# Local attention with memory readout and a gated MLP: the order of issue written out as a table, and five settings of steps

## The chip, the core and the metric

The kernel runs on one core of one Trainium2 chip. The core's engines each take their instructions in the order in which the program lists them: TensorE (PE in the profile, with its weight loads as PEld), VectorE (DVE), ScalarE (ACT), GpSimd (POOL) and SyncE (SP, which here only issues transfers). An instruction that waits for another engine or for a transfer holds back all that stands behind it on its own engine. The metric is the device time of one execution in microseconds, the median of several runs.

## The reference

Attention over B=4 batches, H=8 heads, S=576 positions and D=64, mixed with a readout of a memory matrix, and then a gated MLP over the 2304 tokens:

```python
scores = where(causal, -1e9, q @ k.T / sqrt(D))
a = exp(scores - scores.max(-1)); a /= a.sum(-1) + 1e-9
local = a @ v
q_p = where(q > 0, q, exp(q) - 1) + 1                      # phi
mem_out = (q_p @ M_prev) / ((q_p @ z_prev) + 1e-6)
x = g * mem_out + (1 - g) * local                          # g = sigmoid(beta), by head
xn = x / sqrt(mean(x * x) + 1e-6) * rms_g                  # x as 2304 x 512
out = (silu(xn @ w_gate) * (xn @ w_val)) @ w_out           # 512 -> 1536 -> 512
```

The inputs come as float64 words for the weights and float32 for q, k, v; the result is float32.

## The kernel before

The 2304 tokens are 18 row blocks of 128, numbered in the order in which they are worked on: 0 to 3 are the first rows of the four batches, 4 to 9 are rows 1 to 3 of batches 0 and 1 in turn, 10 holds the 64 last rows of both, 11 to 13 are rows 1 to 3 of batch 2, 14 to 16 those of batch 3, 17 the last rows of both. Two blocks make one of nine chunks of 256 tokens for the MLP. Blocks 0 to 3 and chunk 0 are computed in float32; all later ones split each operand into a high and a low float16 part and add three matmuls.

Attention goes by units of one block and one or two heads (four in blocks 0 to 3). A unit's score matmuls (`u_scores`, L480) are masked, scaled and reduced to a row minimum by DVE (L486); ACT takes the exponential (L545) and writes the high part of P (L547); the low part P lo is a subtraction (`u_lo`): on DVE (L563), or on POOL (L567) for the blocks that `NPOOL` names, of which those that get a P lo are 4 to 7. On POOL's way a small DVE addition (L494) shifts the row minimum first. Then the SP queue issues one transposing transfer for both parts (PT, L569), and TensorE multiplies it with v (`u_pv`, L600 to L602). The score banks (tag sc) and the gate/value banks (tag gv) in PSUM have two buffers each, PT has four.

For each block q, k, phi(q) and x are split into two parts and transposed by transfers on the SP queue (qT, kT, phT, xT); qT needs two more copies inside SBUF (L385, L386), which wait in the queue for its transpose. v is split by `prep_v` with `VWAY`: "1" is a scaling pass and a cast on ACT (L125, L129) and a subtraction on POOL (L132); "0" is one scaling cast on ACT (L108) and a multiply-subtract on DVE (L111).

The MLP of a chunk has twelve gate/value projections (`m_proj`, 24 matmuls L959 each, or L952 in float32 in chunk 0) and twelve down projections (`m_down`, L1029 to L1031). `m_act` (L975, L976, L979) turns a projection's bank into h and so frees it. The weights are converted from float64 words (L871, L875, L881) and split (L111) during the first chunks; `C1` is how many pieces of the second third of d_ff are converted ahead of the first projections, `E0` how many projections of chunk 1 go ahead of the split of w_out.

The statistics of a batch need gram matmuls (`gram`, csum, L167); `GDE` names, for the first two batches, the event that they are held back for (x0 and x1: the RMS scale of block 0 and of block 1 is done). The preparation of a block is a list of steps (st), each emitted at a place that a planner chooses by costs; `o` shifts some steps of the second rows of batches 2 and 3. The program is emitted in that planner's order with priorities, and the framework's scheduler sets the final order on each engine by those priorities and its own estimate of times.

Of the kernel before, what the change touches and what calls it, by code (L numbers as in the profile page):

```python
# [29 lines left out]
SP = ((2, 0), (2, 4))  # L30
GDE = ("x1", "x1")
GDL = ("x1", "x1")
# [3 lines left out]
T32 = "aaadd"  # L36
C1 = 8
E0 = 8
HEADA = 0.4
D1 = 4  # L40
D2 = 8
SPLIT = ("0", "0", "033", "0")
VWAY = "11"
HLAG = 3
# [22 lines left out]
GP = -600  # L67
NPOOL = (2, 8)


@with_exitstack
def attn_memory_moe_kernel(
# [12 lines left out]
    nc = tc.nc  # L85
# [4 lines left out]
    P = 128  # L90
# [13 lines left out]
    ps = ctx.enter_context(tc.tile_pool(name="ps", bufs=2, space=bass.MemoryType.PSUM))  # L104


    def hi_cast(dst, src, scale):
# [26 lines left out]
    def pow2_scales(ssq, n, s_out, inv_out):  # L134
# [9 lines left out]
        nc.vector.reciprocal(s_out, inv_out)  # L144

    def over_partitions(src, n):

        t = ps.tile([P, 512], F32, tag="sc", name="allp")
        nc.tensor.matmul(t[:n, :P], src, ident, start=True, stop=True)
        v = tiny.tile([P, 1], F32, tag="vmax", name="vmax", bufs=1)  # L150
        nc.vector.tensor_reduce(v[:n], t[:n, :P], axis=AX.X, op=ALU.max)
        nc.tensor.matmul(t[:, P : P + n], v[:n].to_broadcast([n, P]), ident[:n, :n], start=True, stop=True)
        return t[:, P : P + n]

    def total(src, n):

        t = ps.tile([P, 512], F32, tag="sc", name="allp")
        nc.tensor.matmul(t[:, :n], mhalf[:, 1:2].to_broadcast([P, P]), src, start=True, stop=True)
        return t[:, :n]
# [65 lines left out]
    zs = const.tile([P, 4], F32, name="zs")  # L225

    def load_kv(n, ev=""):
        tag = "kvt" if is_tail[n] else "kv"
        stage[n] = sb.tile([P, 2, HD], F32, tag=tag, name=f"kv{n}", bufs=1 if is_tail[n] else 4)
        for j in range(2):  # L230
            ins = nc.sync.dma_start(out=stage[n][:, j], in_=qkv[at_row[n], :, j, :])
            if ev:
                after(ins, event[ev])


    def load_M(b):
        if b < 2:
            held["M", b, 0] = held["M", b, 1] = NF - b + 100
            qst[("M", b)] = wo[:, NF - b, :]
        else:  # L240
            qst[("M", b)] = sb.tile([P, HD], F32, tag="q", name=f"M{b}")
        for hf in range(2):
            nc.sync.dma_start(
                out=qst[("M", b)][hf * D : (hf + 1) * D], in_=M_prev[b].rearrange("d h e -> d (h e)")
            )
# [3 lines left out]
    def spare(name):  # L249
        t = sb.tile([P, H, VW], F16, tag="v16", name=name, bufs=10)  # L250
        return t.bitcast(F32).rearrange("p a b -> p (a b)")[:, :HD]

    def load_32(n):
        kv32[n] = []
        for j in range(2):
            kv32[n].append(spare(f"kv32_{n}_{j}"))
            nc.sync.dma_start(out=kv32[n][j], in_=qkv[at_row[n], :, j, :])
        b = blocks[n][0]
        qst["M32", b] = spare(f"M32_{b}")
        for hf in range(2):  # L260
            nc.sync.dma_start(
                out=qst["M32", b][hf * D : (hf + 1) * D], in_=M_prev[b].rearrange("d h e -> d (h e)")
            )

    def src32(n, j):
        return stage[n][:, j] if n < 2 else kv32[n][j]

    def load_q(n):
        if n in qst:
            return  # L270
        qst[n] = sb.tile([P, HD], F32, tag="q", name=f"q{n}")
        nc.sync.dma_start(out=qst[n], in_=qkv[at_row[n], :, 2, :])
# [7 lines left out]
    def stat_begin(b):  # L280
        stt[b] = tiny.tile([P, 3, NI + 1], F32, tag="stt", name=f"stt{b}", bufs=2)
        nc.gpsimd.memset(stt[b], 0.0)

    def stat_blk(b, i):
        if b < 2:
# [18 lines left out]
        else:  # L304
            n = blk_of[(b - b % 2, NI)]
            r0 = (b % 2) * TR
            for j in range(2):
                square_acc(stage[n][r0 : r0 + TR, j], stt[b][r0 : r0 + TR, j, NI : NI + 1])

    def stat_M(b):  # L310

# [5 lines left out]
        del held["M", b, 0]  # L317

    def stat_end(b):
        if b >= 2:  # L320
# [16 lines left out]
        if b % 2 == 1:  # L337
# [3 lines left out]
            tcb[b // 2] = t  # L341

    def prep_M(b):
        src = (qst.pop if b >= 2 else qst.get)(("M", b)).rearrange("p (h e) -> p h e", h=H)
# [21 lines left out]
    qsc = {}  # L366

    def q_stats(n):
        ss = tiny.tile([P, 2], F32, tag="ss", name="ss", bufs=2)
# [4 lines left out]
        pow2_scales(ss, 2, sc[:, 0:2], sc[:, 2:4])  # L374

    def q_consts(n):
        c, sc = consts_of(n), qsc[n]

        nc.vector.tensor_tensor(sc[:, 4:6], sc[:, 1:3], c[:, 6:8], ALU.mult)

    def prep_q(n):
        t = split_rows(qst[n], qsc[n][:, 0:1], RWAY[0])
# [3 lines left out]
        nc.sync.dma_start(out=qT[n][:D, 1], in_=qT[n][D:, 0])  # L386

    def phi_calc(n):

# [6 lines left out]
        qst[n] = ph  # L396

    def prep_phi(n):
        t = split_rows(qst.pop(n), qsc[n][:, 1:2], RWAY[1])
        phT[n] = sb.tile([P, H, P], F16, tag="phT", name=f"phT{n}", bufs=1)  # L400
        tposed(phT[n], t)

    def transposed(dst, src, on_act):

# [18 lines left out]
    def prep_qk32(n):  # L423
# [3 lines left out]
        transposed(q32[n][:, 0], qst[n], T32[1] == "a")  # L427

    def prep_phi32(n):
        transposed(q32[n][:, 1], qst.pop(n), T32[2] == "a")  # L430

    def prep_k(n):
        c = consts_of(n)
        t = split_rows(stage[n][:, 0], c[:, 0:1], RWAY[2])
        kT[n] = sb.tile([P, H, P], F16, tag="kT", name=f"kT{n}", bufs=10)
        tposed(kT[n], t)

    def prep_v(n):
        c = consts_of(n)
# [9 lines left out]
    def group(n):  # L449
        return max(1, 4 // (blocks[n][1] + 1)) if blocks[n][1] < 2 else 1  # L450

    def u_scores(n, h0):
        b, i = blocks[n]
# [43 lines left out]
    def tail_scores(n, h, s, nm, t, w):  # L497
# [29 lines left out]
        Ssb[(n, h)] = (s, w + P, nm0)  # L527

    def u_exp(n, h0):
        s, w, nm = Ssb[(n, h0)]  # L530
# [12 lines left out]
        for g in range(G):  # L543
            v_ = s[:, g * w : (g + 1) * w]
            nc.scalar.activation(v_, v_, AF.Exp, bias=nm[:, g : g + 1], scale=-1.0)  # L545
        p16 = sb.tile([P, 2 * (NI * P + P)], F16, tag="P16", name="P16", bufs=2)
        nc.scalar.activation(  # L547
            p16[:, : G * w], s[:, : G * w], AF.Copy, scale=PSCALE if not lo_on_pool(n, h0) else 1.0
# [3 lines left out]
    def lo_on_pool(n, h0):  # L552
        return NPOOL[0] <= n < NPOOL[1]

    def u_lo(n, h0):
        if n < NA:
# [17 lines left out]
    def after(ins, ev):  # L574
# [4 lines left out]
        )  # L579

    def u_pv(n, h0):
        b, i = blocks[n]
# [40 lines left out]
    pairs = {}  # L623

    def pair_memory(pr):

# [9 lines left out]
        pairs[pr] = mb, zb  # L636

    def pair_M(b):

# [5 lines left out]
        if b < 2:  # L645
            del held["M", b, 1]

    def mem32(n):

# [17 lines left out]
        nc.vector.tensor_tensor(t1s[n], acc, f.unsqueeze(2).to_broadcast([P, H, D]), ALU.mult)  # L667

    def pv32(n, h0, pt):
        b, i = blocks[n]  # L670
        if h0 == 0:
            accs[n] = ps.tile([P, 2, 4, D], F32, tag="a1", name=f"loc{n}", bufs=1)
        for g in range(group(n)):
# [5 lines left out]
            )  # L679

    def evac32(n, g4):
        f = den.pop((n, g4))
# [10 lines left out]
        event["e%d%d" % (n, g4)] = nc.gpsimd.tensor_tensor(part, part, t2, ALU.add)  # L693

    def mem_mm(n, g4):
        if n < NA:
# [23 lines left out]
        for (bb, r), acc in zip(halves, found):  # L720
# [4 lines left out]
            )  # L725

    def loc_evac(n, g4):
        if n < NA:
# [27 lines left out]
    xdone = {}  # L756

    def x_norm(n):
        x = t1s[n].rearrange("p h d -> p (h d)")
# [6 lines left out]
        t1s[n] = (x, ss)  # L766

    def x_float(n):

# [11 lines left out]
        )  # L781

    def x_split(n):
        if n < 2:
# [36 lines left out]
    def hold(p, at):  # L821
# [3 lines left out]
        return wo[:, at : at + 2, :].rearrange("p a f -> p (a f)")  # L825

    def load_w(m, cc, t):
        w = (w_gate, w_val)[m]
# [11 lines left out]
    def in_wgv(at):  # L840
        return wgv[:, at : at + 2, :].rearrange("p a f -> p (a f)")

    def load_pre(b, i):

        pre[(b, i)] = []
        for j in range(2):
# [4 lines left out]
            pre[(b, i)].append(t)  # L851

    def load_wo(f):
        at = {0: 7, 1: 9, 2: 11, 3: 7, 4: 9, 5: 11, 7: 9, 9: 11}.get(f)
# [9 lines left out]
    event = {}  # L864

    def f64_to_f32(raw, dst, p):

# [21 lines left out]
    wos = const.tile([P, NT3 + 8], F32, name="wos")  # L889

    def gv_scales(t):

# [23 lines left out]
        )  # L916

    def wo_scales():

# [7 lines left out]


    def w_split(m, cc, t):
        p = piece(m, cc, t)  # L930
        src = wgv[:, p + 1, :]
        sc = rgs[:, t, m, cc : cc + 1]
        split(wgv16[:, p, :512], wgv16[:, p, 512:], src, sc, way_of(SPLIT, t, p % (2 * NC)))

    def wo_split(f):
        src = wo[:, f + 1, :]
# [3 lines left out]
    gvp, h16s, outp = {}, {}, {}  # L940

    def m_proj(F, m):
        c, f = F // NF, F % NF
# [4 lines left out]
        for cc in range(NC):  # L948
# [9 lines left out]
            for lhs, rhs in ((whi, cc), (whi, NC + cc), (wlo, cc)):  # L958
                nc.tensor.matmul(o, lhs, xT[c][:, rhs, :], start=(cnt == 0), stop=(cnt == 3 * NC - 1))  # L959
                cnt += 1  # L960

    def m_act(F):
        if F < NF:
# [19 lines left out]
        h16s[F] = th  # L983

    def m_split(F):
        if F < NF:
# [10 lines left out]
        h16s[F] = h16  # L997

    def put(c, tb, scale):
        if tb == 0:  # L1000
# [7 lines left out]
        for p0, np_, b, s0 in rows_of(2 * c + tb):  # L1008
            (nc.scalar).dma_start(out=out[b * S + s0 : b * S + s0 + np_, :], in_=res[p0 : p0 + np_])

    def m_down(F):
        c, f = F // NF, F % NF
# [21 lines left out]


    def setup_small():
        nc.scalar.dma_start(out=beta_sb, in_=beta.rearrange("(o h) -> o h", o=1).to_broadcast([P, H]))
# [4 lines left out]
    gmax2 = const.tile([P, 1], F32, name="gmax2")  # L1042

    def setup_gain():

# [3 lines left out]
        nc.vector.tensor_tensor(gmax2, gmax2, gmax2, ALU.mult)  # L1049

    def setup_consts():

# [21 lines left out]
    def prep_steps(n):  # L1074

        b, i = blocks[n]
        st = [[] for _ in range(8)]
        o = 2 if i == 1 and b >= 2 else 0
        if n < NA:
# [138 lines left out]


    def w_conv(i):  # L1220
        m, cc, t = pcs[i]
# [3 lines left out]
        for nx in NEXT.get(i, ()):  # L1225
            load_w(*pcs[nx])

    def wo_conv(f):
        f64_to_f32(raws.pop(("o", f)), wo[:, 1 + f, :], len(pcs) + f)
# [88 lines left out]
    a_until(1e9)  # L1318
    downs(NCHUNK * NF, 99)


# [59 lines left out]
```

## Time and profile before

| | us |
|---|---|
| median of 3 runs | 638.47 |
| the runs | 644.07, 637.28, 638.47 |
| the profiled execution | 637.33 |
| its span in the trace | 635.5 |
| PE busy | 600.3 |
| DVE busy | 444.5 |
| ACT busy | 405.3 |
| POOL busy | 175.3 |

The span is the time between the first and the last recorded instruction; the profiled execution's own time is 1.8 us longer. The busy time of PE counts the modelled ends of pipelined matmuls. Idle time of an engine is put down to whatever ended it.

### The profile page before, as it was taken

The page shows a single profiled execution, that of the slowest core. Times are in us where ns is not written, and L with a number is a line of the kernel's source. Part 1 is how long each engine was busy: PE and PEld are TensorE (multiplying, and loading weights), DVE is VectorE, ACT ScalarE, POOL GpSimd, SP SyncE. Part 2 cuts the span into 40 slices and gives each one's busy share as a digit, 9 for nine tenths or more (in the row PEclk, how much of TensorE's full clock was granted, in tenths as well). Part 3 has the DMA queues.
Part 4 walks back from the last instruction along what each step waited for, and adds up shares of the span by engine and source line. Part 5 has one row for each costly group of instructions (what it writes and reads, how often), then busy time and mean ns, then how long its engine had stood idle before and what let it go on. Part 6 is the DMA issues. An engine that isn't in the chain of part 4 may idle for free. (4 is left out here: it accounts for less than half of the span.)

```text
span 635.5 us, 15913 instructions
## 1 busy us (share of the span) xinstructions
PE 600.3 (94%) x6092; PEld 473.0 (74%) x6092; DVE 444.5 (70%) x1301; ACT 405.3 (64%) x874; POOL 175.3 (28%) x263
## 2 busy tenths in 40 slices
PE   5889999998899999999999988889999999999996
PEld 4778876777667788888778766667777878887774
DVE  3858886887997668676977667687876757852222
ACT  4687994978887667675755664886665645432321
POOL 2220010228865343222212521152222222022111
PEclk9969999999999999999999999999999999999999
DMA  7996652478877776785597467549856444430001
GB/s 254 352 393 248 224 188 83 77 177 192 159 144 155 133 153 145 145 167 90 61 179 144 96 132 151 130 88 177 161 109 112 85 85 92 80 64 18 34 1 34
DMA packets 183788, 87.58 MB, mean 138 GB/s; under 512 B 165792, under 2 KB 165792, under 8 KB 183712
## 3 DMA queue, kind: packets, MB, share of 16 engines
q1 hardware_dynamic: 180640, 81.82, 57.9%
q10 hardware_dynamic: 3072, 4.74, 2.4%
q8 instruction: 48, 0.79, 0.5%
q14 instruction: 28, 0.23, 0.1%
HBM read 37.77 MB, written 4.72 MB: 67 GB/s over the span
## 5 line engine op out<-in xcount | busy, mean ns | idle before, releaser
L959 PE MATMUL gv<-xT,wgv 128*128 128x256 f16 x2304 | 322.2, 273 | 2.8 <-DVE th L979 2.7
L959 PEld LDWEIGHTS <-wgv 128*128 128x128 f16 x2304 | 220.4, 98 | 39.8 <-issue 3.7
L996 POOL TENSOR_TENSOR h<-th,h 128x256 f16<-128x256 f32 x88 | 64.8, 737 | 253.3 <-ACT h L995 247.0
L545 ACT ACTIVATE S<-S,nm 128x256 f32<-128x256 f32 (+3 forms) x112 | 70.2, 639 | 45.5 <-DVE nm L486 33.6
L480 PE MATMUL sc<-kT,qT 128*128 128x128 f16 x576 | 87.1, 219 | 3.3 <-DMA qT<-qT 1.6
L976 DVE SCALAR_TENSOR_TENSOR th<-th,gv 128x256 f32<-128x256 f32 x96 | 40.0, 417 | 59.0 <-ACT th L975 58.2
L975 ACT ACTIVATE th<-gv,wt 128x256 f32<-128x256 f32 x96 | 44.6, 464 | 50.3 <-PE gv L959 43.9
L486 DVE CUSTOM_DVE_ANT_0 S<-sc,mask,qsc 128x256 f32<-128x256 f32 (+2 forms) x96 | 57.4, 612 | 15.2 <-PE sc L480 12.9
L1029 PE MATMUL out<-wo,h 128*128 128x512 f16 x176 | 66.6, 379 | 0.5 <-ACT h L995 0.5
L1030 PE MATMUL out<-wo,h 128*128 128x512 f16 x176 | 66.7, 379 | 0.0
L547 ACT ACTIVATE P<-S 128x512 f16<-128x512 f32 (+2 forms) x96 | 58.2, 607 | 12.7 <-DMA PT<-P 10.7
L1031 PE MATMUL out<-wo,h 128*128 128x512 f16 x176 | 65.7, 379 | 0.0
L563 DVE SCALAR_TENSOR_TENSOR P<-S,P 128x512 f16<-128x512 f32 (+2 forms) x72 | 51.3, 712 | 20.6 <-ACT P L547 20.0
L995 ACT CAST h<-th 128x256 f16<-128x256 f32 x88 | 35.1, 399 | 45.4 <-DVE th L979 37.6
L480 PEld LDWEIGHTS <-qT 128*128 128x128 f16 x576 | 50.8, 98 | 9.2 <-issue 3.9
L600 PE MATMUL loc<-v,PT 128*128 128x65 f16 x288 | 48.6, 193 | 6.6 <-DMA PT<-P 5.8
L602 PE MATMUL loc<-v,PT 128*128 128x65 f16 x288 | 48.5, 193 | 0.0
L601 PE MATMUL loc<-v,PT 128*128 128x64 f16 x288 | 48.2, 193 | 0.0
L979 DVE SCALAR_TENSOR_TENSOR th<-th,wt,gv 128x256 f32<-128x256 f32 x96 | 45.8, 477 | 2.1
L952 PE MATMUL gv<-xT,wgv 128*128 128x256 f32 x192 | 46.5, 397 | 0.8 <-DVE xT L779 0.8
L952 PEld LDWEIGHTS gv<-xT,wgv 128*128 128x128 f32 x192 | 37.3, 199 | 7.4 <-DVE xT L779 1.1
L600 PEld LDWEIGHTS <-PT 128*128 128x128 f16 x288 | 27.7, 97 | 13.1 <-DMA PT<-P 8.5
(233 smaller groups left out, 1181.2 us busy)
## 6 DMA issues: line engine op xcount, KB each, us to landing
kv<-in_qkv_dram SPq DMA_DIRECT2D x40, 256.0 KB, 3.9
q<-in_qkv_dram SPq DMA_DIRECT2D x18, 256.0 KB, 3.6
wo<-in_moe_w_out_dram SPq DMA_DIRECT2D x8, 512.0 KB, 3.8
out_dram<-res ACTq DMA_DIRECT2D x16, 256.0 KB, 2.7
wgv<-in_moe_w_val_dram SPq DMA_DIRECT2D x7, 512.0 KB, 8.9
wo<-in_moe_w_gate_dram SPq DMA_DIRECT2D x7, 512.0 KB, 8.0
qT<-qT SPq DMA_DIRECT2D x28, 128.0 KB, 2.4
wgv<-in_moe_w_gate_dram SPq DMA_DIRECT2D x5, 512.0 KB, 7.3
```

Of the source, the lines that this page charges most:

```text
L480: nc.tensor.matmul(t[:, g * w + j * P : g * w + (j + 1) * P], qT[n][:, t2, h, :], kT[blk_of[(b, j)]][:, h, :], start=(t2 == 0), stop=(t2 = ...
L486: nc.vector.tensor_tensor_reduce(out=s[:, g * w : (g + 1) * w], in0=t[:, g * w : (g + 1) * w], in1=mask[:, m0 : m0 + w], scale=qsc[n][:, 5 ...
L545: nc.scalar.activation(v_, v_, AF.Exp, bias=nm[:, g : g + 1], scale=-1.0)
L547: nc.scalar.activation(p16[:, : G * w], s[:, : G * w], AF.Copy, scale=PSCALE if not lo_on_pool(n, h0) else 1.0)
L563: m = nc.vector.scalar_tensor_tensor(out=p16[:, w : 2 * w], in0=s[:, :w], scalar=PSCALE, in1=p16[:, :w], op0=ALU.mult, op1=ALU.subtract)
L600: nc.tensor.matmul(a, phi_, vhi, start=(j == 0), stop=False)
L952: nc.tensor.matmul(o, wgv[:, 1 + p, o0 : o0 + P], xT[0][:, cc, :], start=(cc == 0), stop=(cc == NC - 1))
L959: nc.tensor.matmul(o, lhs, xT[c][:, rhs, :], start=(cnt == 0), stop=(cnt == 3 * NC - 1))
L996: nc.gpsimd.tensor_tensor(h16[:, 1], th, h16[:, 0], ALU.subtract)
L1029: nc.tensor.matmul(o, hh, whi, start=(f == 0), stop=False)
L1030: nc.tensor.matmul(o, hh, wlo, start=False, stop=False)
L1031: nc.tensor.matmul(o, hl, whi, start=False, stop=(f == NF - 1))
```

## The change

Functions that emit instructions get a decorator, `@keep("S")` and the like, which notes under a letter and the engine each instruction that they emit. At the end `issue_in_order` goes through a table of strings, one for each engine: a letter takes the next instruction noted under it, a number after it that many, and "~k" skips k of them. Each instruction is tied to the one before it in the string by an order-only dependency. So the table, not the scheduler, sets the order on PE, ACT, DVE, POOL and SP; the strings were made for transfers of twice the length. What is computed, and each instruction, stays, but for five settings: GDE for batch 0, C1, E0, VWAY, NPOOL, and besides them the 2 in `o`.

```diff
-GDE = ("x1", "x1")
+GDE = ("x0", "x1")
...
-C1 = 8
-E0 = 8
+C1 = 4
+E0 = 4
...
-VWAY = "11"
+VWAY = "00"
...
-NPOOL = (2, 8)
+NPOOL = (0, 0)
+
+ISSUE = {
+    "PE": (
+        "T8ZZ~1T8ZT4SS~1S~2S~3Zu4T4S5S~1S~2S~3T4S4u2Tu2Th4T4u4~4T2hTh3T2u4Th8ss~3ss~2ss~1s2R8G4G4~4GG~3GZG~2G3Z~1GZT4ZT4"
...
+    ),
...
+    lanes, labels, seen = {}, ["."], [0]
+
+    def sort_in():
+
+        have = nc.cur_bb.bb.instructions
+        for ins in have[seen[0] :]:
+            lanes.setdefault((ins.engine, labels[-1]), []).append(ins)
+        seen[0] = len(have)
+
+    def keep(kind):
+
+        def wrap(fn):
+            def go(*p, **k):
+                sort_in()
+                labels.append(kind)
+                got = fn(*p, **k)
+                sort_in()
+                labels.pop()
+                return got
+
+            return go
+
+        return wrap
+
+    def issue_in_order():
+
+        sort_in()
+        for name, text in ISSUE.items():
+            last = None
+            for kind, count, skip in re.findall(r"([^\d~])(\d*)(?:~(\d+))?", text):
+                for _ in range(int(count or 1)):
+                    ins = lanes[getattr(mybir.EngineType, name), kind].pop(int(skip or 0))
+                    if last is not None:
+                        tc.add_manual_dep(
+                            ins, last.name,
+                            mybir.DependencyInfo(mybir.DependencyClass.NoSync, mybir.DependencyReason.DATA),
+                            reason="order",
+                        )
+                    last = ins
...
+    @keep("S")
     def u_scores(n, h0):
...
-        nc.scalar.activation(
+        keep("C")(nc.scalar.activation)(
...
-        o = 2 if i == 1 and b >= 2 else 0
+        o = 1 if i == 1 and b >= 2 else 0
...
     downs(NCHUNK * NF, 99)
+    issue_in_order()
```

Three places of the two orders follow. Lines are those of each kernel's own file, and numbers behind a name tell buffers apart.

ACT in the head, around the squares of blocks 0 and 1 (junk, xs) and the phi exponential of block 2 (ph); before:

```order
L537 ACTIVATE S,den<-S,nm 128x128 x16
L277 ACTIVATE junk,xs<-t_0_326 128x512
L391 ACTIVATE ph<-q_198 128x512
L277 ACTIVATE junk,xs<-t_1_341 128x512
L871 ACTIVATE wgv<-wgv 128x512
```

and with the change:

```order
L666 ACTIVATE S,den<-S,nm 128x128 x12
L391 ACTIVATE junk,xs<-t_0_326 128x512
L391 ACTIVATE junk,xs<-t_1_341 128x512
L513 ACTIVATE ph<-q_198 128x512
L1016 ACTIVATE wgv<-wgv 128x512
```

The square of block 1 has moved ahead of block 2's exponential.

DVE among the scores of block 5 (S, nm), the gate steps (th) and P lo; before:

```order
L494 TENSOR_SCALAR nm_1648<-nm_1648 128x2
L976 SCALAR_TENSOR_TENSOR th_1575<-th_1575,gv14_1530 128x256
L979 SCALAR_TENSOR_TENSOR th_1575<-th_1575,wt_90,gv14_1530 128x256
L111 SCALAR_TENSOR_TENSOR wgv_84<-wgv_84,rgs_83 128x512
L486 ISA S_1716,nm_1717<-sc_1718,mask_73,qsc_1497 128x256
```

and with the change, from the same scores of block 5 (S_1716 before, S_1708 now):

```order
L614 ISA S_1708,nm_1709<-sc_1710,mask_73,qsc_1493 128x256
L614 ISA nm_1709 128x1
L260 TENSOR_REDUCE vmax_1806<-allp_1804 1x1
L219 SCALAR_TENSOR_TENSOR v16_5_1623<-kv5_836,cb1_492,v16_5_1623 128x8x64
L219 SCALAR_TENSOR_TENSOR v16_6_1951<-kv6_1343,cb0_466,v16_6_1951 128x8x64
L219 SCALAR_TENSOR_TENSOR wgv_84<-wgv_84,rgs_83 128x512
L1127 SCALAR_TENSOR_TENSOR th_1704<-th_1704,gv15_1627 128x256
L693 SCALAR_TENSOR_TENSOR P16_1604<-S_1579,P16_1604 128x512
L1130 SCALAR_TENSOR_TENSOR th_1704<-th_1704,wt_90,gv15_1627 128x256
```

The additions to nm are gone, and two v splits and a P lo (L693) of block 4 stand on DVE between the gate steps.

SP around the units of block 12 and the preparation of block 13; before:

```order
L363 DMA_TRANSPOSE phT12_5772<-row16_5769 128x8x128
L272 DMA q14_6296<-in_qkv_dram 128x512
L569 DMA_TRANSPOSE PT_5903<-P16_5806 128x6x128
L569 DMA_TRANSPOSE PT_5964<-P16_5906 128x6x128
L363 DMA_TRANSPOSE qT13_5940<-row16_5937 128x8x128
L793 DMA_TRANSPOSE xT5_5668<-x16_6020 128x8x128
L385 DMA qT13_5940<-qT13_5940 64x1024
L386 DMA qT13_5940<-qT13_5940 64x1024
L569 DMA_TRANSPOSE PT_6075<-P16_5980 128x6x128
```

and with the change:

```order
L481 DMA_TRANSPOSE phT12_5727<-row16_5724 128x8x128
L481 DMA_TRANSPOSE qT13_5904<-row16_5901 128x8x128
L355 DMA M3_6361<-in_M_prev_dram 64x512
L934 DMA_TRANSPOSE xT5_5633<-x16_5984 128x8x128
L699 DMA_TRANSPOSE PT_5867<-P16_5770 128x6x128
L506 DMA qT13_5904<-qT13_5904 64x1024
L507 DMA qT13_5904<-qT13_5904 64x1024
L699 DMA_TRANSPOSE PT_5928<-P16_5870 128x6x128
L481 DMA_TRANSPOSE kT13_6073<-row16_6070 128x8x128
```

The transpose of qT13 stands ahead of block 12's first two PTs instead of behind them, and its two copies between these two.

## Rows read from the trace of the kernel before

**Rows 1.** The engines' totals: busy us, share of the span, instructions.

```profile
PE 600.3 (94%) x6092; PEld 473.0 (74%) x6092; DVE 444.5 (70%) x1301; ACT 405.3 (64%) x874; POOL 175.3 (28%) x263
```

**Rows 2.** By stretch: length; busy PE, PEld, DVE, ACT, POOL; clock, DMA share, GB/s.

```profile
0.00:40.00 40.00, 28.43 (x176) 24.55 (x177) 24.16 (x98) 25.25 (x71) 12.43 (x33) 0.89 0.93 318
40.00:140.00 100.00, 99.33 (x645) 76.63 (x644) 79.80 (x264) 81.08 (x184) 10.69 (x18) 0.99 0.60 185
140.00:200.00 60.00, 54.59 (x587) 41.78 (x586) 54.88 (x159) 51.97 (x111) 40.96 (x50) 1.00 0.81 165
200.00:360.00 160.00, 158.04 (x1897) 127.25 (x1895) 119.39 (x335) 106.42 (x221) 50.27 (x75) 1.00 0.71 132
360.00:440.00 80.00, 69.44 (x767) 53.36 (x765) 57.00 (x162) 53.59 (x114) 20.59 (x28) 1.00 0.68 130
440.00:630.00 190.00, 189.93 (x2029) 149.29 (x2026) 108.52 (x287) 86.27 (x175) 40.33 (x60) 1.00 0.38 76
```

**Rows 3.** PE's waits, 340 to 440: us in total, times, longest.

```profile
PE loc L600 <- DMA PT<-P: 4.8, 5, 1.6
PE mem L711 <- DMA phT<-row: 1.8, 1, 1.8
PE gv L959 <- DVE th L979: 1.4, 1, 1.4
```

**Rows 4.** PE's waits, 100 to 215.

```profile
PE sc L480 <- DMA qT<-qT: 1.6, 1, 1.6
...
PE out L1030 <- DVE wo L111: 1.3, 2, 0.8
PE loc L600 <- DMA PT<-P: 1.0, 2, 0.8
```

**Rows 5.** Transfers: issues, and median us from issue to landing.

```profile
PT<-P SPq DMA_TRANSPOSE x96, 3.2
```

**Rows 6.** PE's timeline at 374: start, length, idle before.

```profile
374.70 1.47 PE L959 MATMUL gv<-xT,wgv 128*128 128x256 f16 x12
```

**Rows 7.** Instructions by form: count, busy us, mean ns, idle before.

```profile
L132 POOL TENSOR_TENSOR v<-kv,v 128x512 f16<-128x512 f32 x18 | 21.2, 1188 | 14.6 <-ACT v L129 14.6
...
L563 DVE SCALAR_TENSOR_TENSOR P<-S,P 128x512 f16<-128x512 f32 x40 | 28.7, 719 | 14.0 <-ACT P L547 13.8
...
L567 POOL TENSOR_TENSOR P<-S,P 128x384 f16<-128x384 f32 x16 | 16.0, 1007 | 21.2 <-ACT P L547 21.2
...
L567 POOL TENSOR_TENSOR P<-S,P 128x512 f16<-128x512 f32 x8 | 9.5, 1187 | 2.6 <-ACT P L547 2.2 <-PE gv L959 0.4
L563 DVE SCALAR_TENSOR_TENSOR P<-S,P 128x384 f16<-128x384 f32 x16 | 8.9, 554 | 1.9 <-ACT P L547 1.8
...
L494 DVE TENSOR_SCALAR nm<-nm 128x2 f32<-128x2 f32 x8 | 3.0, 376 | 0.1
```

**Rows 8.** DVE by form, 140 to 200.

```profile
L111 DVE SCALAR_TENSOR_TENSOR wo<-wo,wos 128x512 f16<-128x512 f32 x12 | 11.9, 992 | 0.0
...
L393 DVE SCALAR_TENSOR_TENSOR ph<-q,ph 128x512 f32<-128x512 f32 x2 | 2.9, 1438 | 0.1
```

**Rows 9.** DVE by form, 220 to 300.

```profile
L111 DVE SCALAR_TENSOR_TENSOR row<-ph,qsc,row 128x512 f16<-128x512 f32 x3 | 2.3, 751 | 3.9 <-ACT row L108 3.9
...
L393 DVE SCALAR_TENSOR_TENSOR ph<-q,ph 128x512 f32<-128x512 f32 x2 | 1.7, 868 | 0.0
```

**Rows 10.** PE's timeline in the head, 32 to 54.

```profile
32.83 1.04 PE L167 MATMUL csum<-kv 128*128 128x128 bf16 x8 [2.53 <-POOL xs L765]
...
46.30 0.38 PE L149 MATMUL allp<-ident,ssm 128*1 128x128 f32 x2
...
53.96 1.16 PE L469 MATMUL sc<-k,q 64*128 64x128 f32 x16
```

**Rows 11.** ACT's timeline at 30.

```profile
30.25 0.63 ACT L391 ACTIVATE ph<-q 128x512 f32<-128x512 f32 x1 [2.87 <-POOL t L693]
```

**Rows 12.** The stretch 32 to 41, columns as in Rows 2.

```profile
32.00:41.00 9.00, 7.34 (x26) 5.98 (x27) 5.83 (x10) 9.00 (x19) 4.05 (x7) 0.50 1.04 381
```

## What I expect of it, and why

> **What bounds the kernel now.** I read the engine totals first: TensorE is busy 600.3 of 635.5 us, 94%, and no engine that computes beside it passes 70% [rows 1]. The change leaves TensorE's 5846 matmuls as they are, so only its idle time can move. Second, the table by stretches says where that idle time lies [rows 2]: stretch minus PE busy is 11.6 us up to 40 us, 0.7 in 40–140, 5.4 in 140–200, 2.0 in 200–360, 10.6 in 360–440 and 0.07 in the 190 us after that, 30.3 in all. The reader is to see two islands, 140–200 and 360–440, between stretches that are full. Third, the waits name what ended the idle time there. In 340–440 it is the transposed probabilities (PT) before a unit's first PV matmul, 4.8 us in 5 waits, the transposed phi of block 12, 1.8, and a PSUM bank that the DVE step of the gate projection frees late, 1.4 [rows 3]. In 100–215 it is a mixed bag: qT, wo, PT, each 1 to 2 us [rows 4]. All of these are ends of chains over ACT, DVE and the SP queue, whose transposes take 3.2 us to land [rows 5]. The island in 360–440 has DVE and ACT at 57 and 54 of 80 us [rows 2], so it is one of order: the PV is issued too soon after its scores.
>
> **The table, 360–440.** Order of issue sets how much PE work stands between a unit's last score matmul and its first PV. Counted in the two orders, block 12's eight units had 37 to 69 gate/value matmuls there and now have 51 to 81; besides them 12 to 18 down-projection matmuls, now 17 to 19. Block 13's had 39 to 91, now 68 to 108. Twelve gate/value matmuls in a row take 1.47 us, so (1.47-0.27)/11 = 0.11 us each [rows 6]. The shortest of block 12's gaps gets 14 x 0.11 = 1.5 us from these alone, and its last one (37 to 81) 4.8 us; the longest of the five PT waits is 1.6 us [rows 3]. I let 1.3 of the 4.8 us stand, for the units whose gap grows least. The SP queue agrees half: between qT13's transpose and the two copies that wait for it stood one transfer, now three, so the copies hold the queue less long; but block 12's second PT now stands behind them, where it was the third. By the count of PE work ahead of them, phi of block 12 is read 3 us later than before (the wait of 1.8 us goes), and the bank of gv65 is asked for some 6 us after its last user instead of 2 (1.4 goes). So 4.8-1.3+1.8+1.4 = 6.7 of the 10.6 us go; of the other waits, each 0.7 or less, I leave all, and round to **-6.5 us**. Bounds: 0, if every release is late by what the gap grew, and -10.6, all of the idle.
>
> **NPOOL and VWAY, 140–200.** The P lo of blocks 4 to 7, 16 of 1.007 us and 8 of 1.187 on POOL, becomes 16 of 0.554 and 8 of 0.719 on DVE [rows 7], 14.6 us in all, and 24 small additions (L494) go, of which the eight wide ones were 3.0 us; I leave the narrow ones out. The v split of 18 blocks loses 1.188 us of POOL and one ACT pass each, and gets a DVE step of the form of L111, 0.75 [rows 7, 9]: 13.5. Over the run DVE gets 14.6+13.5-3.0 = 25.1 us and POOL loses 16.0+9.5+21.2 = 46.7. In most stretches DVE's part is hidden under TensorE: DVE was busy 119 of 160 us in 200–360 and 108 of 190 after 440 [rows 2]. It isn't hidden in 140–200, where DVE was busy 54.9 of 60 us. There stood 14 of the 24 P lo, 7 v splits and all the wide L494: 8 x 0.719 + 6 x 0.554 + 7 x 0.75 - 3.0 = +11.3 us, so 66.2 of 60 at the durations shown.
>
> Against that stands what POOL did to DVE. In 140–200, with POOL busy 41 us, the wo split of L111 took 992 ns and phi's L393 1438 [rows 8]; in 220–300, with POOL lightly used, the same forms took 751 and 868 [rows 9]. Twelve times 0.24, twice 0.57, and an estimated 1.5 us in the other forms make about 5.5 us, and most of POOL's work there leaves: DVE comes to about 60.7 of 60. [...]
>
> The other cover is room before 140, where the new settings (C1 and E0 4 instead of 8) and the table place some weight and v splits earlier: DVE had 79.8 of 100 us in 40–140 [rows 2]. The gaps on PE grow a little too: blocks 6 and 7 had 45 to 72 gate/value matmuls between scores and PV, now 50 to 84. Gap against load, I take **-1 us**, with bounds -5.4 (all idle goes) and +13 (the slow rival).
>
> **GDE and the head.** The gram of kv0 (8 csum matmuls, 1.04 us) stood behind a wait of 2.53 us for the second block's xs; with event x0 it goes ahead of both xtp groups and so into that wait [rows 10]: -1.0 us. ACT's square for x1 now goes ahead of block 2's phi exponential, 0.63 us [rows 11], which takes up to 0.5 us more off that wait. Against it: between the first two projections and block 2's scores stood 7.7 us of grams and transposes (46.3 to 53.96 us [rows 10]); now only 8 gram matmuls and the transposes do, so the scores come up before ACT's copies of k and q, and I expect a wait of 1.5 to 2.5 us. The grams come later, so their work is not lost. Sum **+0.5 us**. [...]
>
> The o setting (2 to 1) moves two batches' preparation by a step inside the table's order and is in the counts above. From about 490 us on both orders are the same, the tail too: 0 there.
>
> **Sum**: -6.5-1+0.5 = -7 against the profiled execution's 637.33 us, so 630.3. That execution lies 0.2% under the median of the runs, 638.47; I forecast 630. A difference below 1% (632.1 to 644.9) is about what a measurement of this kernel can't tell from none.
>
> **Rivals.**
> *The waits only move* (no change): with PV later, its PT buffers (4) and the score banks (2) come free later, and the next scores wait instead. For: only two of the six rows in rows 3 and 4 are PT; the chains are many. Against: after 440 us the same buffers run 190 us with 0.07 us of idle [rows 2]. It keeps 3 to 6 of the 6.5 us and gives 634 to 637.
>
> *DVE becomes the bound in 140–200* (slower): a P lo on DVE waits at the head of the queue for ACT's P and holds everything behind it, the steps that free gate banks and the wo splits. The 56 P lo in rows 7 had 14.0+1.9 us of such idle, 0.28 us each; 24 more make 6.7 us. If the relief from POOL doesn't come, DVE needs 66.2+6.7 = 72.9 of 60 us: +12.9 us, and the time is 637.3+12.9+0.5-6.5 = 644, or 651 if 360–440 keeps its waits too. It decides when DVE needs more than some 64 of 60 us there. For: DVE is already 91% busy in that stretch. Against: 20 us of room in 40–140, and the lengthened L111 and L393. [...]
>
> *Both islands go* (larger gain): -10.6-5.4-1.6 = -17.6 gives 620. For: if POOL held DVE up for all of the time that leaves it in 140–200, 8 x 1.187 + 6 x 1.007 + 7 x 1.188 = 24 us, DVE would need 42 of 60, and chains over DVE would be early. Against: the four waits of rows 3 and 4 that I let go or stay sit in different chains, and the lengthening seen is 5.5 us.
>
> *The change doesn't do what it says*: its table was made for transfers twice as long, so the longer gaps could lie where none is needed. That is so for blocks 8 to 11, whose gaps hardly change, and after 490 us, but not for blocks 12 and 13. It would give 637, and is counted with the first rival.
>
> **Chances.** The forecast, 624 to 634: 0.45. The waits only move, 634 to 642: 0.26. Slower through DVE, 640 to 651: 0.17. Larger gain, 616 to 624: 0.12. Of the forecast's 0.45 about 0.37 lies below 632.1; with the larger gain, faster has 0.49. Slower by over 1% has 0.13: two thirds of the DVE case and a little for a bad head. The rest, 0.38, is within 1%. The range 619 to 643 leaves out about 0.05 below and 0.14 above.
>
> **What will show it.** Right: idle of PE in 360–440 below 5 us, no PT wait over 1 us there; P lo x96 on DVE at about 0.7 us; the wo split of L111 in 140–200 nearer to 750 ns than to 992; nothing different after 490 us. Wrong: DVE above 58 of 60 us about 140–200 with PE waits on PT or th there; a new wait of over 2 us near 45–55 us with the clock at 0.50 behind it; waits for score banks in 360–440.

## The result, and the profile after

The change takes 621.61 us, median of 622.36, 620.85, 620.02 and 629.44; the kernel before took 640.07 beside it. The ratio is 0.968, 95% interval 0.962 to 0.975: 3.2% faster, where 1.3% was forecast. The direction was right, the size was not, and the time is nearly that of the rival "both islands go" (620). The times of one kernel can fall into two groups some 9 us apart, which seem to go with the pace of PE in the first 45 us (last section; in the traces of e1 to e4, e6, e7, e10, e12 and e13 it is the longer one, with 147 to 161 matmuls up to 40 us against 174 to 188 in the others), so stretches behind 140 us, lowest runs, or lower with lower and upper with upper runs are compared below.

The profiled execution took 622.36 us, its span 620.6, that of before 635.5: 15.0 us less. Of the changed kernel first the totals, then the stretches (length; busy us and count of PE, PEld, DVE, ACT, POOL; clock, DMA share, GB/s), as in [rows 1, 2].

```profile
PE 598.5 (96%) x6092; PEld 474.6 (76%) x6092; DVE 451.1 (73%) x1319; ACT 396.8 (64%) x856; POOL 136.6 (22%) x221
```

```profile
0.00:40.00 40.00, 28.52 (x174) 24.88 (x175) 22.00 (x95) 23.19 (x66) 13.79 (x34) 0.97 0.90 308
40.00:140.00 100.00, 98.79 (x645) 76.42 (x644) 80.71 (x262) 80.58 (x184) 9.86 (x16) 0.99 0.59 186
140.00:200.00 60.00, 57.80 (x613) 44.46 (x610) 59.28 (x175) 52.15 (x111) 19.36 (x30) 1.00 0.86 161
200.00:360.00 160.00, 159.56 (x1929) 129.38 (x1927) 125.53 (x347) 103.87 (x217) 38.81 (x61) 1.00 0.76 138
360.00:440.00 80.00, 78.17 (x865) 61.99 (x864) 63.70 (x183) 58.41 (x125) 18.49 (x28) 1.00 0.79 144
440.00:610.00 170.00, 170.00 (x1847) 134.39 (x1846) 98.26 (x258) 77.09 (x154) 34.92 (x52) 1.00 0.42 76
```

Stretch minus PE busy is PE's idle time: 8.7 us less in 360–440 (10.6 to 1.8), 3.2 less in 140–200 (5.4 to 2.2), 1.5 less in 200–360 (2.0 to 0.4), and 0.4 more up to 140 (12.3 to 12.7). That is 13.0 of the 15.0 us; PE's own busy total fell by 1.8. DVE in 140–200 is full, 59.3 of 60 us, and PE lost little by it: of its waits in 100–215, 0.5 us are for DVE's wo and 0.2 for th.

PE's waits in 340–440 of the changed kernel (us in total, times, longest); against [rows 3] the phi and gate waits are gone, and of PT's 0.3 us is left:

```profile
PE allp L268 <- DVE mx L441: 1.0, 1, 1.0
PE sc L608 <- DVE nm L614: 0.5, 1, 0.5
PE loc L731 <- DMA PT<-P: 0.3, 1, 0.3
```

DVE's forms in 140–200 (count, busy us, mean ns, idle before):

```profile
L219 DVE SCALAR_TENSOR_TENSOR wo<-wo,wos 128x512 f16<-128x512 f32 x12 | 9.4, 780 | 0.0
...
L693 DVE SCALAR_TENSOR_TENSOR P<-S,P 128x512 f16<-128x512 f32 x8 | 5.7, 712 | 0.2 <-ACT P L190 0.2
...
L219 DVE SCALAR_TENSOR_TENSOR v<-kv,cb,v 128x512 f16<-128x512 f32 x5 | 4.5, 917 | 0.0
...
L693 DVE SCALAR_TENSOR_TENSOR P<-S,P 128x384 f16<-128x384 f32 x6 | 4.0, 672 | 0.0
...
L515 DVE SCALAR_TENSOR_TENSOR ph<-q,ph 128x512 f32<-128x512 f32 x2 | 1.4, 686 | 0.0
...
L219 DVE SCALAR_TENSOR_TENSOR v<-kv,tcb,v 128x512 f16<-128x512 f32 x1 | 0.7, 740 | 0.0
```

All 14 P lo have come to DVE, 6 v splits where I counted 7, and with POOL at 19.4 us instead of 41.0 the wo split takes 780 ns and phi's step 686, against 992 and 1438 [rows 8]. Five of the v splits took 917 ns, not the 750 that I had put.

Another place where the two traces part in 360–440 is SP. Of the kernel before, the SP queue around the transpose of qT and the two copies that wait for it (start, length, line, transfer):

```profile
362.10 1.28 SPq L363 DMA_TRANSPOSE qT<-row  x1
363.44 1.31 SPq L363 DMA_TRANSPOSE kT<-row  x1
365.44 0.49 SPq L385 DMA_DIRECT2D qT<-qT  x1
365.98 0.59 SPq L386 DMA_DIRECT2D qT<-qT  x1
366.66 0.54 SPq L231 DMA_DIRECT2D kv<-in_qkv_dram  x1
367.30 1.24 SPq L793 DMA_TRANSPOSE xT<-x  x1
368.59 0.57 SPq L231 DMA_DIRECT2D kv<-in_qkv_dram  x1
```

and of the changed kernel:

```profile
358.04 1.29 SPq L481 DMA_TRANSPOSE qT<-row  x1
359.37 1.32 SPq L481 DMA_TRANSPOSE kT<-row  x1
360.75 1.06 SPq L342 DMA_DIRECT2D kv<-in_qkv_dram  x2
361.86 0.43 SPq L386 DMA_DIRECT2D q<-in_qkv_dram  x1
362.39 0.49 SPq L506 DMA_DIRECT2D qT<-qT  x1
362.92 0.59 SPq L507 DMA_DIRECT2D qT<-qT  x1
```

The loads of kv now go into the time in which the copies wait for qT, 2.7 us after its transpose instead of 4.6 and 6.5. ACT's squares of kv (junk) feel it. ACT's timeline of before:

```profile
369.68 0.63 ACT L277 ACTIVATE junk<-kv 128x512 bf16<-128x512 f32 x1 [1.30 <-DMA kv<-in_qkv_dram]
...
373.32 0.63 ACT L277 ACTIVATE junk<-kv 128x512 bf16<-128x512 f32 x1 [2.92 <-DMA kv<-in_qkv_dram]
```

and of the changed kernel:

```profile
363.86 0.63 ACT L391 ACTIVATE junk<-kv 128x512 bf16<-128x512 f32 x1 [0.28 <-DMA kv<-in_qkv_dram]
...
364.71 0.63 ACT L391 ACTIVATE junk<-kv 128x512 bf16<-128x512 f32 x1
```

Two holes of ACT's in-order queue, 4.2 us together, have become 0.3.

### The profile page after: what moved, and what is told of

Same layout as the page of the kernel before. It is cut to its first block, busy times and chain, and to the rows that moved or that the text cites. A ratio compares the mean times of both kernels' runs of the same rounds, so it can differ in the third digit from the quotient of the medians.

```text
span 620.6 us, 15845 instructions
## 1 busy us (share of the span) xinstructions
PE 598.5 (96%) x6092; PEld 474.6 (76%) x6092; DVE 451.1 (73%) x1319; ACT 396.8 (64%) x856; POOL 136.6 (22%) x221
## 5 line engine op out<-in xcount | busy, mean ns | idle before, releaser
L1109 PE MATMUL gv<-xT,wgv 128*128 128x256 f16 x2304 | 312.6, 273 | 0.7 <-DMA xT<-x 0.5
L608 PE MATMUL sc<-kT,qT 128*128 128x128 f16 x576 | 79.3, 220 | 0.8 <-DVE nm L614 0.5
L693 DVE SCALAR_TENSOR_TENSOR P<-S,P 128x512 f16<-128x512 f32 (+2 forms) x96 | 67.4, 703 | 17.4 <-ACT P L190 16.8
L614 DVE CUSTOM_DVE_ANT_0 S<-sc,mask,qsc 128x256 f32<-128x256 f32 (+2 forms) x96 | 57.4, 610 | 17.2 <-PE sc L608 16.7
L190 ACT ACTIVATE P<-S 128x512 f16<-128x512 f32 (+2 forms) x96 | 58.0, 605 | 12.7 <-DMA PT<-P 10.7
L608 PEld LDWEIGHTS <-qT 128*128 128x128 f16 x576 | 48.3, 98 | 7.3 <-issue 1.8
L731 PE MATMUL loc<-v,PT 128*128 128x65 f16 x288 | 40.9, 193 | 1.0 <-DMA PT<-P 1.0
L733 PE MATMUL loc<-v,PT 128*128 128x65 f16 x288 | 41.2, 193 | 0.0
L732 PE MATMUL loc<-v,PT 128*128 128x64 f16 x288 | 40.6, 194 | 0.0
L1185 PEld LDWEIGHTS <-h 128*128 128x128 f16 x176 | 17.1, 98 | 19.5
```

Of the source, the lines that this page charges most:

```text
L190: got = fn(*p, **k)
L608: nc.tensor.matmul(t[:, g * w + j * P : g * w + (j + 1) * P], qT[n][:, t2, h, :], kT[blk_of[(b, j)]][:, h, :], start=(t2 == 0), stop=(t2 = ...
L614: nc.vector.tensor_tensor_reduce(out=s[:, g * w : (g + 1) * w], in0=t[:, g * w : (g + 1) * w], in1=mask[:, m0 : m0 + w], scale=qsc[n][:, 5 ...
L693: m = nc.vector.scalar_tensor_tensor(out=p16[:, w : 2 * w], in0=s[:, :w], scalar=PSCALE, in1=p16[:, :w], op0=ALU.mult, op1=ALU.subtract)
L732: nc.tensor.matmul(a[:, :D], phi_, vlo, start=False, stop=False)
L1185: nc.tensor.matmul(o, hl, whi, start=False, stop=(f == NF - 1))
```

## The experiments

One table first; the sections say what each run is. Idle is stretch minus busy of PE in the profiled execution, in us. The kernel before ran beside each group of runs, with a lowest time of 637.28 beside the change, 636.68 beside e1 to e4, 634.84 beside e5 to e8, 635.71 beside e9 to e12 and 635.26 beside e13 and e14; so times of different groups compare to some 2 us.

| run | median, us | lowest | ratio, 95% | idle 140–200 | idle 360–440 |
|---|---|---|---|---|---|
| the change | 621.61 | 620.02 | 0.968 [0.962, 0.975] | 2.2 | 1.8 |
| e1 | 641.03 | 636.33 | 1.002 [0.994, 1.010] | 4.7 | 8.6 |
| e2 | 634.35 | 629.65 | 0.989 [0.981, 0.998] | 5.4 | 5.9 |
| e3 | 657.54 | 654.22 | 1.027 [1.021, 1.033] | 9.1 | 8.3 |
| e4 | 627.52 | 623.38 | 0.980 [0.974, 0.986] | 5.0 | 1.5 |
| e5 | 638.39 | 627.24 | none | 5.1 | 6.0 |
| e6 | 629.88 | 623.92 | 0.985 [0.975, 0.994] | 2.9 | 0.9 |
| e7 | 648.73 | 645.26 | 1.017 [1.009, 1.024] | 6.7 | 10.8 |
| e8 | 620.38 | 619.57 | 0.972 [0.968, 0.977] | 3.3 | 0.9 |
| e9 | 668.41 | 665.72 | 1.045 [1.040, 1.051] | 6.3 | 14.4 |
| e10 | 671.49 | 666.22 | 1.048 [1.041, 1.055] | 5.8 | 14.5 |
| e11 | 627.61 | 625.75 | 0.983 [0.978, 0.988] | 3.0 | 3.8 |
| e12 | 682.05 | 677.93 | 1.067 [1.060, 1.075] | 8.2 | 15.8 |
| e13 | 630.98 | 629.54 | 0.992 [0.988, 0.997] | 3.1 | 6.9 |
| e14 | 620.44 | 618.20 | 0.973 [0.970, 0.976] | 2.1 | 3.3 |

**Order or settings (e1, e2, e3).** e1 writes the order of before as a table and takes from the change only the two settings that move splits:

```diff
-VWAY = "11"
+VWAY = "00"
-NPOOL = (2, 8)
+NPOOL = (0, 0)
```

> The order of the kernel before, written as a table, with only NPOOL and VWAY new (P lo of blocks 4 to 7 and the v splits on DVE, at the place where POOL did them). If the gain is one of order (A), the two islands stay: idle of PE 10 us in 360-440, 5 us or more in 140-200, time 636 to 641. If taking POOL's work out of 140-200 is what emptied that island (B), PE's idle there falls to 2 to 3 us and the time is 633 to 636, with 360-440 as before. If DVE is the bound there without the new order (C, the slow rival of the prediction), 140-200 loses 5 us or more: 643 to 648.

It gave no change in time, with both islands there (A). e2 is the other half: the change's table on PE, ACT, DVE and SP, the v passes of before put in their places, POOL left to the scheduler.

```diff
-VWAY = "00"
+VWAY = "11"
-NPOOL = (0, 0)
+NPOOL = (2, 8)
```

> The change with NPOOL and VWAY of before: P lo of blocks 4 to 7 and the v splits on POOL again, in the new order on PE, ACT, DVE and SP, POOL free. (A) order alone: 620 to 624, PE idle under 3 us in both islands. (B) split alone matters in 140-200: idle there 4 to 6 us, time 624 to 627; 360-440 as in the change (under 2.5 us).

It kept a third of the gain, with both islands there, which neither (A) nor (B) had. By the lowest runs the kernel before is at 634.84 (lowest of 21 runs beside e1 to e12), e1 at 636.33, e2 at 629.65 and the change at 620.02: the new splits alone bring nothing, the new order alone 5 us, the two together 15 (7 and 17 against the runs of before beside each). e3 takes the five settings and o without a table:

```diff
-    issue_in_order()
```

> All five settings and o of the change, no table: the scheduler orders the engines. (A) 633 to 642, with PE idle of 8 us or more in 360-440. If the settings carry the gain without the table: 621 to 628.

It was 2.7% slower, worse than either expectation, with PE waits of up to 2.5 us in 340–440: the settings alone are no gain in the scheduler's order.

**Where in the program (e4, e8).** e4 uses the order of before up to 270 us and the change's behind it, with the new splits.

```diff
-GDE = ("x0", "x1")
+GDE = ("x1", "x1")
-C1 = 4
-E0 = 4
+C1 = 8
+E0 = 8
```

> The order of before up to 270 us of its trace and the change's order after that; NPOOL and VWAY new, the rest of the head as before. If the island in 360-440 is worth what the two traces show, 10 us, the time is 10 us less than e1's, and PE idle in 360-440 is under 2.5 us. If the island in 360-440 needs the earlier stretches too (arrears from 140-200), 4 us or more of idle stay there.

The second island went as with the whole change (1.5 us of idle), the first stayed. e8 keeps the change's settings and has the order of before up to 100 us only; its strings differ from the change's in their first parts alone.

> The change with the order of before up to 100 us of its trace, and the change's order behind that; GDE stays x0, so the gram of kv0 no longer waits for xs. The change's head is 1.5 to 2 us behind before's at equal work (a 2.9 us wait of the second xtp behind phi's DVE steps, and 1 us of copies of k and q). If that is its order, the time is 617 to 620 against 620 to 622; if the new order behind 100 us needs its own head, 622 or more.

At 620.38 it is level with the change (619.57 to 621.41 against three runs of 620.02 to 622.36): the new order of the head is worth nothing or costs up to 1 us. It is the best median in the table, by less than runs of the change scatter.

**My step, the PE distance from scores to PV (e7).** In the order of before, with all its settings, each PV that PE issued between 355 and 432 us goes behind 24 further matmuls. The piece of PE's string where it begins (P is PV, G gate/value, D down, S scores):

```diff
-...MGMGMD6G5P20GPGPGPGPG15DP8SS~5P4D5G17PS10GP...
+...MGMGMD6G24DSS~5D2P20DPDPDPGPG16P8S2P4S8G7D6GPG2S6...
```

> The kernel before with its own order as a table, but every PV matmul of blocks 12 and 13 behind 24 more of the other matmuls, 2.6 us of gate/value work; nothing else moves. If the distance from scores to PV is the cause, the PT waits in 340-440 fall from 4.8 us to under 1.5 and the time by 3 to 4 us; phi, the gate bank and the rest stay at 4 to 6 us of idle. If PV's delay only moves the wait (PT buffers, banks), the idle in 360-440 stays at 9 us or more and the time within 1 us.

It was 1.7% slower. PE's waits of this kernel in 340–440:

```profile
PE allp L275 <- DVE mx L448: 3.2, 1, 3.2
PE gv L1116 <- DVE th L1137: 2.2, 3, 1.3
PE mem L855 <- DMA phT<-row: 2.0, 1, 2.0
PE sc L615 <- DMA qT<-row: 1.5, 1, 1.5
PE sc L615 <- DVE nm L621: 1.3, 3, 0.6
PE loc L738 <- DMA PT<-P: 0.4, 1, 0.4
```

PT fell from 4.8 us [rows 3] to 0.4, just as my step had it, and the idle time did not fall: 10.8 us. The wait moved to whatever was late next. PT's waits were where the lateness showed, not what made it.

**The SP queue (e9, e10, e12, e11).** e9 gives the kernel before the change's SP order from 270 us on and leaves the other engines; in its string (r is a block's qT transpose, then its two copies; k, F and X the transposes kT, phT and xT; l the loads of kv, b that of q, m one of M; L a PT):

```diff
-...L5XLrbkr2Ll2L2kLFbL3l2L2rkr2lXlFbL2rXr2LkL...
+...L5XrbLr2kl2L3kLFbL3l2L2rkl2br2XFrmXLr2LkF...
```

> The kernel before with its own order as a table, and the change's order on the SP queue alone from 270 us on: kv and q loads of the next blocks stand ahead of the copies of qT that wait in the queue. Theory D: ACT stood at the head of its queue for late transfers in 350-440 (7.8 us for kv before its squares), and the later PT waits followed. Then ACT's wait for kv falls below 4 us, PE idle in 360-440 from 10.6 to 5 to 8, and the time by 3 to 5 us. Theory A (PE's own order): ACT's wait falls, but PE idle stays at 9 us or more.

It was 4.5% slower: transfers stood at the head of the queue before their operands were made, and held all behind them. Two rows of SP's waits in 340–440:

```profile
SPq L705 <- DVE P L699: 29.1, 8, 10.7
SPq L487 <- DVE x L225: 10.2, 1, 10.2
```

The first of them was 22.8 us in 12 waits, at most 5.9, in the kernel before. PE's longest wait for PT grew to 5.6 us. e10 is the same with the new splits, e12 the same with e7's later PV.

> The same new SP order from 270 us on, over e1 (old order elsewhere, NPOOL and VWAY new). If SP's order and the one ACT pass per v are two halves of the same cure, PE idle in 360-440 is 3 to 5 us and the time 5 to 8 us under e1's; if the orders of PE, ACT and DVE are needed too, idle stays at 7 us or more.

> e9 with the PV of blocks 12 and 13 behind 24 more matmuls as in e7. e7 alone was worse than before, since what ACT and the gate banks waited for came later too. If late transfers were the cause of that, the two together give 360-440 under 5 us of idle and 4 to 7 us less than before; if PV's delay itself moves the waits, it is worse than e9 by 3 us or more.

e10 was as slow as e9 (their intervals overlap) and e12 slower still: SP's part of the table without the rest gives none of its gain. So I went the other way and undid one thing in the change. e11 puts a stretch of nine letters about 360 us, seven of which change places, back into the order that before had, kv's loads behind the copies:

```diff
-...L3l2L2rkl2br2XFrmXLr2...
+...L3l2L2rkr2lXlFbrmXLr2...
```

> The change with nine transfers of the SP queue about 360 us in the order of before: the two copies of qT12 ahead of the two loads of kv15, the load of q14 last. Theory D: ACT waits 2 to 4 us more at the squares of kv15 and q14, and PE idle in 360-400 grows by 1 to 4 us; time 622 to 625 against 620 to 622. If the change's longer distance on PE hides 4 us of delay, the time does not move.

In the profile 2.0 us of idle time came back in 360–440, and with it ACT's wait for kv (345 to 440):

```profile
ACT junk L392 <- DMA kv<-in_qkv_dram: 5.5, 3, 3.4
```

against 2.5 us in 3 waits, at most 1.2, in the change. The profiled executions are 3.4 us apart, the medians 6.0, more than expected. These places are one shown piece of the 8.7 us.

**The splits in the new order (e5, e6, e13, e14).** In the change, e5 undoes VWAY, e6 NPOOL.

```diff
-VWAY = "00"
+VWAY = "11"
```

> The change with VWAY alone undone (v split: two passes on ACT and a subtraction on POOL; the order on PE, ACT, DVE and SP that of the change, POOL free). If ACT's second pass is what e2 lost in 360-440 (five v splits in a row held ACT 6.6 us there), that island has 4 us or more of PE idle again and the time is 625 to 629 against 620 to 622 of the change's undisturbed runs. If NPOOL carries what e2 lost, the time stays at 620 to 623.

```diff
-NPOOL = (0, 0)
+NPOOL = (2, 8)
```

> The change with NPOOL alone undone (P lo of blocks 4 to 7 on POOL with the additions to nm; the same order, POOL free). If POOL's P lo is what e2 lost in 140-200: 4 to 6 us of PE idle there, 624 to 626; 360-440 stays under 2.5 us. If VWAY carries it all: 620 to 622 and under 3 us of idle in 140-200.

With VWAY undone both islands are back, 5.1 and 6.0 us (its runs are 627.24 and three of 638.28 to 638.69, too far apart for a ratio: the one is 5 to 7 us above the change's lower three, the three are 9 above its 629.44). With NPOOL undone they are not, 2.9 and 0.9, although POOL was busy 36 of 60 us in 140–200 and the wo split took 959 ns: by the idle time there NPOOL is worth less than 1 us. The median of 629.88 lies outside both expectations, but up to 610 us PE is idle 17.4 us in e6's trace and 17.2 in the change's; what parts the two is PE's busy total, 606.0 against 598.5 us, where its first 140 us did 753 matmuls in e6 and 819 in the change. e6's one low run, 623.92, is 1.6 to 3.9 us above the change's lower three, so by the times NPOOL could be worth up to 4 us.

VWAY does two things: it takes one pass of each v off ACT, and moves the low part from POOL to DVE. e13 adds the pass alone to the change, multiplying v by 1 in place, where the old way had it:

```diff
-VWAY = "00"
+VWAY = "88"
...
+        if way == "8":
+            nc.scalar.activation(src, src, AF.Copy, scale=1.0)
+            way = "0"
```

> The change, with one more pass on ACT ahead of each of the 18 v splits, placed where the old way had its scaling pass; it multiplies v by 1 in place. DVE, POOL, PE and SP keep the change's order. Theory A (undoing VWAY cost 9 us because each v holds the ACT queue for two passes instead of one): 629 to 633, PE idle of 4 us or more in each of 140-200 and 360-440 again. Theory B (it cost them because the low part of v came by way of POOL and landed later): 620 to 624, idle there as with the change, 2.2 and 1.8 us.

e14 moves the low part alone, with POOL's order free; POOL subtracts from the unscaled v, so the low part of v is another number:

```diff
-VWAY = "00"
+VWAY = "99"
...
+        if way == "9":
+            hi_cast(dst_hi, src, scale)
+            nc.gpsimd.tensor_tensor(dst_lo, src, dst_hi, ALU.subtract)
+            return
```

> The change, with the low part of v made on POOL after a single ACT cast, and POOL's order left to the scheduler, as in the run with VWAY undone; ACT keeps the change's one pass per v. POOL subtracts from the unscaled v, an instruction of the same kind and size as the old one, so the numbers of v's low part are not the reference's. Theory A (the ACT pass is what counts): 620 to 624. Theory B (the way over POOL is what counts): 627 to 632, with PE idle of 4 us or more in 140-200 and in 360-440, and DVE's forms that read two operands longer in 140-200 than with the change.

The two came out cleanly apart. e13: seven of twelve runs at 629.54 to 631.50 and five at 638.38 to 640.38, against 620.02 to 622.36 and 629.44 of the change: 9.5 us more between the medians of the lower runs, and between those of the upper. e14: 620.44. It is the ACT pass; nothing in e13's trace waits for one of the 18 passes itself, so it is the time that they hold ACT. One part of Theory A missed: in 140–200 e13's idle time is 3.1 us, not 4 or more. e13's stretches from 140 to 440:

```profile
140.00:200.00 60.00, 56.95 (x565) 42.94 (x564) 57.17 (x161) 54.05 (x113) 21.67 (x29) 0.97 0.74 143
200.00:360.00 160.00, 157.86 (x1905) 127.24 (x1903) 125.18 (x343) 106.52 (x218) 37.24 (x57) 1.00 0.78 142
360.00:440.00 80.00, 73.09 (x802) 56.80 (x799) 62.03 (x178) 60.38 (x130) 17.37 (x29) 1.00 0.68 127
```

Against the change that is 5.1 us more idle time in 360–440, 1.7 more in 200–360, 0.9 more in 140–200, and there the clock is 0.97 on the mean of the 60 us, worth 0.03 x 60 = 1.8 by estimate: together 9.5. ACT is at 60 of 80 us in 360–440, three quarters. What the pass does is seen where five v stand in a row on ACT between P of one unit and S of the next. The change:

```profile
398.52 0.63 ACT L190 ACTIVATE P<-S 128x512 f16<-128x512 f32 x1 [0.58 <-DMA PT<-P]
399.06 0.71 ACT L216 ACTIVATE M<-M,cb 128x512 f16<-128x512 f32 x1
399.67 2.54 ACT L216 ACTIVATE v<-kv,cb 128x512 f16<-128x512 f32 x4
402.12 0.71 ACT L216 ACTIVATE v<-kv,tcb 128x512 f16<-128x512 f32 x1
402.73 0.70 ACT L674 ACTIVATE S<-S,nm 128x512 f32<-128x512 f32 x1
```

e13, the same place:

```profile
414.66 0.71 ACT L216 ACTIVATE M<-M,cb 128x512 f16<-128x512 f32 x1
415.28 0.61 ACT L227 ACTIVATE kv<-kv 128x512 f32<-128x512 f32 x1
...
421.65 0.71 ACT L677 ACTIVATE S<-S,nm 128x512 f32<-128x512 f32 x1
```

From M to S it is 3.7 us in the one and 7.0 in the other: the exponentials, and with them P, PT and the score banks, stand 3.3 us longer behind splits of v. Right behind it PE is idle 2.5 us in 420–430 of e13, and 0.5 in 400–410 of the change; most of the 2.5 is one wait for a score bank:

```profile
426.18 0.61 PE L611 MATMUL sc<-kT,qT 128*128 128x128 f16 x8 [1.63 <-DVE nm L617]
```

That this idle time comes of the longer run is read from its place; the rest of the 5.1 us lies elsewhere in the stretch and was not followed to single passes.

## Why the prediction was wrong, step by step

- **What bounds the kernel**: right in the main. PE's idle time in two islands was what could move, and nothing changed behind 440 us. Between the traces 15.0 us went where I had 7: 2.2 more in 360–440 and 2.2 more in 140–200 than forecast, 1.5 of idle in 200–360 that I put at nothing, and 1.8 of PE's busy time, where I wrote that "only its idle time can move".
- **The table, 360–440, -6.5 us**: this step failed, in its cause and its size. I had the waits there as "the PV is issued too soon after its scores". Longer distances alone took the PT waits away and left the idle time (e7). The measured -8.7 us came with the later half of the whole table and the new splits (e4, 1.5 us left); SP's order alone (e9), SP's order with the splits (e10) and the splits alone (e1) did not bring it. Undone in the change, two pieces give idle time back: loads ahead of waiting copies on SP (e11, 2.0 us) and one ACT pass less per v (e13, 5.1 us). They were found one at a time and need not add. I had seen SP's copies but priced only PT and the copies, and passed over the loads of kv that moved ahead of them.
- **NPOOL and VWAY, -1 us**: mis-sized, and a term put at nothing. I wrote that each v loses "one ACT pass" and gave it neither a price nor a reason for none; ACT was busy 52 of 60 us and 54 of 80 in the islands [rows 2]. The pass is worth 9.5 us in the change's order (e13; all of VWAY 5 to 9, e5), most of it in 360–440, and NPOOL and VWAY together nothing in the order of before (e1). The idle time in 140–200 fell by 3.2 us; of that 0.9 came back in e13 and 2.9 in e5.
- **DVE's load**: right as a sum. I had 60.7 of 60 us for 140–200, 59.3 were used. The relief that I had put on POOL's leaving came (the wo split at 780 ns, against 992). The slow rival did not happen, even with 0.7 us of DVE left, though my own sign of it, DVE above 58 of 60, did: full as the queue was, PE's waits for th there were 0.2 us.
- **Work moved from POOL to DVE**: for v's low part it made no difference in the time (e14, 620.44 against 621.61); for NPOOL the idle time says less than 1 us (e6) and its times leave up to 4 us open. The gain of VWAY came from ACT (e13).
- **GDE and the head, +0.5 us**: right as a sum, in part by luck. Idle time up to 140 us is 0.4 us more, and the order of before up to 100 us (e8) is level or 1 us better. The wait of 2.53 us [rows 10] has become one of 2.9 for phi's step on DVE, and the scores wait 1.1 us for ACT's copies of q and k where I had 1.5 to 2.5. So a wait like the old one did come back; but the clock behind it was 0.85 in 32–40 and 0.90 in 40–45, together some 3.4 us at 0.50 (twice 0.15 of 8 us and 0.10 of 5), where before had 9 us [rows 12]. At 0.50, in 38–41, PE began 3 or 4 matmuls a us, at 1.00, in 42–46, 6 or 7.
- **The rivals**: "both islands go" is what happened nearly, at a chance of 0.12. I let it hang on POOL's hold on DVE, which is not its cause: with POOL at 20 of 60 us in 140–200 both islands stayed (e1), and with POOL at 36 they went (e6). No run shows its -1.6 for the head: up to 140 us the idle time rose by 0.4. "The waits only move" describes e7, not the change.

What stays open: how the rest of the 8.7 us in 360–440 divides among PE, DVE and SP (no run takes the longer distances on PE out of the change), which of ACT's single passes count in 140–200, and what made PE's busy time 1.8 us less. The three tables with SP's new order under old strings (e9, e10, e12) were slower than both kernels, so SP's part of the order could not be priced by itself.

## What to carry to other kernels

Price an instruction that leaves an in-order queue by what stands behind it, not by that engine's busy share: 18 passes of 0.6 us on an engine at 64% were worth 9.5 us on another. The wait that the profile names last in an island is a symptom until moving it alone shortens the island; look at what all queues do a few us earlier, above all at loads behind a transfer that waits. When an order is written out for all engines, test it by undoing one thing in it; parts of it put into another order tell little.

## What the runs showed of the hardware

PE went at two paces in the first 45 us. Its transposes of S in the first 45 us (count, busy us, mean ns), in the profiled execution of the change, and then of e13, where PE does the same work:

```profile
L531 PE MATMUL tp<-ident,S 128*128 128x128 f32 x16 | 3.2, 284 | 0.0
```

```profile
L534 PE MATMUL tp<-ident,S 128*128 128x128 f32 x16 | 5.1, 422 | 0.0
```

Granted clock of the stretch up to 40 us was 0.97 and 1.00, so the row of the clock does not show it. In e4's execution it showed 0.50 for the 8 us from 24 on, and the same transposes took 429 ns: e13's 422 is within 2% of that, though its row says 1.00. The lowest mean, 284 ns, stands in the traces of the change, e5, e11 and e14.

DVE's wo split in 140–200 was mostly longer where POOL was busier: 780 ns at 19.4 us of POOL (the change), 816 at 28.3 (e14), 959 at 36.3 (e6), 992 at 41.0 (before). Of all 16 traces, 778 to 838 ns stand in nine of the ten with 18 to 28 us of POOL and 913 to 1072 in five of the six with 36 to 42; e3 (998 at 21.2) and e7 (808 at 39.4) go the other way. That POOL's work is what made them longer was not shown, and PE's idle time did not follow these rows: 2.9 us with 959 ns (e6), 2.2 with 780 (the change).

Behind a wait of 1.6 us for a gate bank in e13, PE's granted clock was 0.83 on the mean of the 10 us from 160 on. By estimate that is 0.17 x 10 = 1.7 us of work at 1.00, as much again as the wait.
